# A list schedule's assumed durations are replaced, and the order that follows from them

## The chip, the core and the metric

The kernel runs on one core of a Trainium2 chip. The metric is the device time of one execution in microseconds. The core has five engines that each work through their own instruction queue in program order: TensorE (PE; its weight loads are shown as PEld), VectorE (DVE), ScalarE (ACT), GpSimd (POOL) and SyncE (SP), which issues the transfers. Nothing is reordered at run time, so the order in which the program is written down decides who waits for whom.

## What is computed

Four images of 12,480 tokens and 128 channels go through attention by way of 32 inducing rows, and each token's result goes through a two-layer ELU network with 2,048 hidden features.

```python
def mab(q, kv):                       # scale = 1/sqrt(C)
    s = scale * (q @ kv.transpose(0, 2, 1))
    a = np.exp(s - s.max(-1, keepdims=True))
    a /= a.sum(-1, keepdims=True) + 1e-09
    return a @ kv
h = mab(I, x)                         # 32 rows per image
x = mab(x, h)                         # every token again
h = x @ w_in
g = np.where(h > 0.0, h, np.exp(np.minimum(h, 0.0)) - 1.0)
out = g @ w_out
```

## The kernel before

Each of the four images is cut into 25 blocks of 512 or 480 tokens, in seven groups of two to four blocks. The network dominates. `unit` (lines 846 to 966) does two of a block's 16 feature chunks, so a block has 8 units and the run has 800, numbered through as unit 0 to 799. A unit is this chain:

- L863 on PE: two matmuls into a pair of PSUM banks, `ph`. There are three such pairs.
- L873 on ACT: `e = exp(ph - 1)`.
- L877 on DVE: the ELU's middle, written to `e` (kinds P and N) or back to `ph` (kind D).
- L887 on ACT (P and D): the rounded high part, `gh`.
- For kind P, L903 on POOL shifts `e` by one, and L907 on POOL makes the low part `gl = e - gh`. For kind D, L893 on DVE makes `gl`. For kind N there is only L903.
- L943 on PE: the second layer into a bank `po`. P and D have four matmuls with `gh` and two with `gl`. N has two matmuls in plain fp32.

A block's units are of the kinds P, D, P, D, P, D, P, N (`KINDS`); only the very first block is all N. After a block, L958 on DVE transposes `po` and SP writes it out. While image b goes through the network, the first attention step of image b+1 runs beside it: L536 makes scores, L595 and L600 their exponentials, and `gather` (L604 to L638) sums the tokens with 32-column matmuls at L614, in pieces of four (`HH`), into `ps_hh`. `attend` (L748 on) does the second attention step, one group ahead of its blocks, with L763 on PE, L787, L802 and L822 on POOL, and DMAs at L832 that put the result into one of six homes `stk`. The last image has no next image beside it.

Before the first unit there is a head of some 76 us: the first image is loaded, transposed (L1020, L1031) and gathered, `weight_steps` (L416 to L478) unpacks 64-bit weights on DVE, ACT and POOL, and a single first block is attended to (the `True` tiles, up to L814), while 64 matmuls called `warm` (L1042) fill PE.

Nothing of the order is written out by hand. Every step is registered with `add(engine, key, hold, ...)`, where `hold` is the duration that the planner assumes. `Program.order` (L167) then plays a list schedule: at each turn it takes the engine that can start first, and of that engine's steps that could start within `LOOK` ns of the earliest one it takes the one with the lowest key. `WAKE` is the wait that it assumes between an engine's work and another engine's start on it. The keys are tables of numbers (`KP`, `ATT`, `FH`, `KS`), one set for each kind of step. The resulting sequence is what each engine's queue holds.

```python
LOOK0 = 116.0
LOOKS = {'PE': 36.0, 'ACT': 105.0, 'DVE': 175.0, 'POOL': 0.0, 'SP': 3411.0}
WAKE = {"PE": 480.0, "ACT": 90.0, "DVE": 90.0, "POOL": 140.0, "SP": 60.0}
def pool_one(n):
    return 0.97 * n + 15, 45.0
def pe(n, passes=1):
    return passes * n / 2.4 + (18 if passes == 1 else 5), 165.0
```

## Time and profile before

| what | value |
|---|---|
| median of 3 runs | 1650.55 us (1650.27 to 1650.57) |
| the profiled execution | 1650.92 us, of which the span from the first to the last instruction is 1649.1 us |
| busy share of the span | PE 99%, POOL 94%, DVE 91%, ACT 90%, PEld 74% |
| granted TensorE clock | 1.00 in every slice |

A busy share is the time in which at least one instruction of the engine is shown as running. The ends of PE's instructions are modelled, and instructions overlap in the pipeline, so PE's pace is read from the distance between the starts of two matmuls, and a wait from a distance that is longer than usual. The same holds for POOL, whose instructions overlap by some 40 ns: the distance of starts is the price, not the shown duration.

### The profile page before, as it was taken

The numbers are of one execution on the slowest core, as the hardware profiler recorded it, in microseconds if no ns is written. First come the engines' busy times: TensorE is split into PE (matmuls) and PEld (weight loads), VectorE is DVE, ScalarE is ACT, GpSimd is POOL, SyncE is SP. The second block draws the span as 40 slices with busy tenths as digits, with TensorE's granted clock in tenths as the row PEclk, the third lists the DMA queues.
The fourth block names the chain that finished last, engine by engine and source line by source line (L and its number), as shares of the span: only waits on it lengthen the run. The fifth ranks groups of instructions, "written<-read, shape, count | busy, mean of one in ns | idle before, by whom it ended". The sixth has DMA issues, their size and how long they took to land.

```text
span 1649.1 us, 23463 instructions
## 1 busy us (share of the span) xinstructions
PE 1626.5 (99%) x7766; PEld 1218.8 (74%) x7766; DVE 1497.5 (91%) x1563; ACT 1485.3 (90%) x1728; POOL 1550.4 (94%) x1051
## 2 busy tenths in 40 slices
PE   6999999999999999999999999999999999999998
PEld 4667777777777777777777777778777777777886
DVE  5899989988999999898899999989989999998986
ACT  6598999899889999989989999999989999999996
POOL 3599999999899999999899999999999999999998
PEclk9999999999999999999999999999999999999999
DMA  8263322312442232321353233221122111111101
...
DMA packets 384186, 97.40 MB, mean 59 GB/s; under 512 B 364672, under 2 KB 370592, under 8 KB 383808
## 3 DMA queue, kind: packets, MB, share of 16 engines
...
## 4 chain that ended last, share of the span: by engine, by line
PE 95%; POOL 1%; DVE 1%; issue 1%; ACT 1%; DMA 1%; SPq 0%; POOLq 0%; DVEq 0%; ACTq 0%
PE po L943 67%; PE ph L863 22%; PE ps_t_False L763 2%; PE ps_s L536 2%; PE ps_hh L614 2%; POOL gl L907 1%; PE warm L1042 1%; POOL e L903 1%; DMA xm<-in_x_dram 1%; PE ps_x L1020 0%; ACT s L595 0%; DVE xT L1031 0%; PE ps_hw L729 0%; DVE e L877 0%; DVE eT L600 0%
## 5 line engine op out<-in xcount | busy, mean ns | idle before, releaser
L907 POOL TENSOR_TENSOR gl<-e,gh 128x1024 fp32r<-128x1024 f32 (+1 forms) x396 | 928.7, 2351 | 16.2
L873 ACT ACTIVATE e<-ph 128x1024 f32<-128x1024 f32 (+1 forms) x800 | 787.4, 1008 | 98.1 <-PE ph L863 93.0
L877 DVE SCALAR_TENSOR_TENSOR e<-ph,e 128x1024 f32<-128x1024 f32 (+1 forms) x503 | 593.8, 1186 | 71.8 <-ACT e L873 67.9
L903 POOL TENSOR_SCALAR e<-e 128x1024 f32<-128x1024 f32 (+1 forms) x503 | 513.7, 1031 | 33.6 <-ACT gh L887 27.8
L943 PE MATMUL po<-gh,wo_h 128*128 128x512 f32 (+1 forms) x1386 | 543.5, 392 | 0.0
L943 PE MATMUL po<-gh,wo_l 128*128 128x512 f32 (+1 forms) x1386 | 536.9, 387 | 0.0
L863 PE MATMUL ph<-stk,hw 128*128 128x512 f32 (+1 forms) x1600 | 510.8, 410 | 2.3 <-DVE e L877 2.1
L887 ACT ACTIVATE gh<-e 128x1024 fp32r<-128x1024 f32 (+1 forms) x396 | 414.2, 1046 | 13.4 <-DVE e L877 12.1
L943 PE MATMUL po<-gl,wo_h 128*128 128x512 f32 (+1 forms) x1386 | 410.4, 394 | 0.5 <-POOL gl L907 0.4
L863 PEld LDWEIGHTS ph<-stk,hw 128*128 128x128 f32 x1600 | 296.9, 188 | 111.1 <-issue 41.6
L877 DVE SCALAR_TENSOR_TENSOR ph<-ph,e 128x1024 f32<-128x1024 f32 (+1 forms) x297 | 355.4, 1197 | 18.5 <-ACT e L873 16.2
L893 DVE SCALAR_TENSOR_TENSOR gl<-ph,gh 128x1024 fp32r<-128x1024 f32 (+1 forms) x297 | 351.5, 1184 | 22.0 <-ACT gh L887 16.5
L943 PEld LDWEIGHTS po<-gl,wo_h 128*128 128x128 f32 x1386 | 256.6, 188 | 73.3 <-issue 14.3
L943 PEld LDWEIGHTS po<-gh,wo_h 128*128 128x128 f32 x1386 | 260.0, 188 | 64.3 <-issue 6.7
L887 ACT ACTIVATE gh<-ph 128x1024 fp32r<-128x1024 f32 (+1 forms) x297 | 299.4, 1008 | 8.5 <-DVE ph L877 7.7
L943 PEld LDWEIGHTS po<-gh,wo_l 128*128 128x128 f32 x1386 | 260.2, 188 | 53.5 <-issue 3.2
L943 PE MATMUL po<-e,wo_n 128*128 128x512 f32 (+1 forms) x396 | 182.1, 582 | 0.0
L943 PEld LDWEIGHTS po<-e,wo_n 128*128 128x128 f32 x396 | 74.3, 189 | 54.5 <-issue 45.8
L958 DVE STREAM_TRANSPOSE o<-po 128x512 f32<-128x512 f32 (+1 forms) x100 | 69.4, 694 | 9.8 <-PE po L943 9.3
L502 DVE STREAM_TRANSPOSE xT<-xq 128x1024 f32<-128x1024 f32 (+2 forms) x39 | 45.1, 1159 | 0.0
L822 POOL TENSOR_TENSOR alo<-aT_False,ahi 128x512 fp32r<-128x512 f32 (+3 forms) x28 | 35.5, 1267 | 0.0
L614 PE MATMUL ps_hh<-xm,eT 128*32 128x128 f32 (+2 forms) x872 | 34.3, 277 | 1.2 <-ACT s L543 0.5
...
## 6 DMA issues: line engine op xcount, KB each, us to landing
...
out_dram<-o SPq DMA_DIRECT2D x160, 60.0 KB, 1.9
...
stk<-ahi SPq DMA_DIRECT2D x80, 60.0 KB, 2.0
...
```

What stands on the lines that cost most here:

```text
L502: add("DVE", key_x, dve(n, True)[0], lambda: nc.vector.transpose(t(), xq().rearrange("p u d -> p (u d)")), r=[(xq, dq) for dq in range(4)] ...
L614: nc.tensor.matmul(ps()[c * Q : (c + 1) * Q, :C], st["e", g]()[:np_, u * Q : (u + 1) * Q], st["xm", g, u - u % UP]()[:np_, u % UP, :], sta ...
L822: add("POOL", at(), pool_two(T)[0], lambda: nc.gpsimd.tensor_sub(alo()[:np_], aT()[:np_], ahi()[:np_].bitcast(F32)), r=[(aT, 0), (ahi, 0)] ...
L863: nc.tensor.matmul(ph()[:, j, :T], st["hw"]()[:, f * P : (f + 1) * P], homes[i][:, :T], start=True, stop=True,)
L873: add("ACT", n + K["exp"][cp], act(2 * T, True)[0], lambda: nc.scalar.activation(e(), ph()[:, :, :T], AF.Exp, bias=-1.0), r=[(ph, 0)], w=[ ...
L877: add("DVE", n + K["mid"][cp], dve(2 * T)[0], lambda: nc.vector.scalar_tensor_tensor(out=ga(), in0=ph()[:, :, :T], scalar=1.0, in1=e(), op ...
L887: add("ACT", n + K["gh"][cp], act(2 * T, how == "D")[0], lambda: nc.scalar.activation(gh(), ga(), AF.Copy, bias=-1.0), r=[(g, 0)], w=[(gh, ...
L893: add("DVE", n + K["gl"][cp], dve(2 * T)[0], lambda: nc.vector.scalar_tensor_tensor(out=gl(), in0=ga(), scalar=-1.0, in1=gh().bitcast(F32) ...
L903: add("POOL", n + K["one"][cp], pool_one(2 * T)[0], lambda: nc.gpsimd.tensor_scalar(out=e(), in0=e(), scalar1=-1.0, scalar2=sign, op0=ALU. ...
L907: add("POOL", n + K["gl"][cp], pool_two(2 * T)[0], lambda: nc.gpsimd.tensor_sub(gl(), e(), gh().bitcast(F32)), r=[(e, 0), (gh, 0)], w=[(gl ...
L943: nc.tensor.matmul(po()[:, :T], w(), g_(), start=po.count == 0, stop=po.count == po.total - 1)
L958: add("DVE", n + K["o"][0], dve(T, True)[0], lambda: nc.vector.transpose(o().rearrange("p u d -> p (u d)"), po()[:, :T]), r=po.parts, w=[( ...
```

## The change

The planner's assumed durations, its assumed waits and its look-ahead get other values, and with them come other keys for the steps of the units, of the next image's attention and of the second attention step. No instruction's work, size or engine changes, and no buffer count does. What changes is only the order in each queue.

```diff
-LOOK0 = 116.0
+LOOK0 = 71.0
...
-LOOKS = {'PE': 36.0, 'ACT': 105.0, 'DVE': 175.0, 'POOL': 0.0, 'SP': 3411.0}
+LOOKS = {'PE': 0.0, 'ACT': 0.0, 'DVE': 72.0, 'POOL': 0.0, 'SP': 4748.0}
...
-FH = {'xq': 113.90625, 'xT': 47.40625, 'ps': 24.640625, 's': -68.828125, 'pm': -3.953125, 'bias': 22.75, 'xm': 48.796875, 'exp': 30.890625, 'eT': 11.796875, 'hh': 12.125, 'h': 70.96875, 'es': 197.71875, 'r': -7.734375, 'hn': 36.515625, 'hT': -31.46875, 'hw': 26.1875}
-ROOM = -31.5625
+FH = {'xq': 94.96875, 'xT': 87.6875, 'ps': 26.15625, 's': -53.15625, 'pm': -29.875, 'bias': 18.1875, 'xm': 112.9375, 'exp': 46.71875, 'eT': -1.328125, 'hh': 5.453125, 'h': 46.1875, 'es': 257.3125, 'r': -13.125, 'hn': 52.296875, 'hT': -78.703125, 'hw': 29.171875}
+ROOM = -32.1875
...
-    WAKE = {"PE": 480.0, "ACT": 90.0, "DVE": 90.0, "POOL": 140.0, "SP": 60.0}
+    WAKE = {"PE": 300.0, "ACT": 70.0, "DVE": 70.0, "POOL": 110.0, "SP": 60.0}
...
 def pool_one(n):
-    return 0.97 * n + 15, 45.0
+    return 0.97 * n + 70, 45.0
...
 def pe(n, passes=1):
-    return passes * n / 2.4 + (18 if passes == 1 else 5), 165.0
+    return passes * n / 2.4 + (16 if passes == 1 else 5), 165.0
...
-        add("ACT", n + K["exp"][cp], act(2 * T, True)[0], lambda: nc.scalar.activation(
+        add("ACT", n + K["exp"][cp], act(2 * T, True)[0] + 12, lambda: nc.scalar.activation(
...
-        add("DVE", n + K["mid"][cp], dve(2 * T)[0], lambda: nc.vector.scalar_tensor_tensor(
+        add("DVE", n + K["mid"][cp], dve(2 * T)[0] + 10, lambda: nc.vector.scalar_tensor_tensor(
...
-                add("ACT", n + K["gh"][cp], act(2 * T, how == "D")[0], lambda: nc.scalar.activation(
+                add("ACT", n + K["gh"][cp], act(2 * T, how == "D")[0] + 20, lambda: nc.scalar.activation(
```

The tables `ATT` (for the groups after the first image's first two) and `KS` (kinds a and l) change throughout, in the same manner as `FH` above.

Three places of the order, before and now. The first is PE's queue near the end of the first image, where the next image's sixth group is gathered (`ps_hh_5`, L614; the numbers in a name count the tile, and `x8` stands for eight matmuls). Before:

```order
L863 MATMUL ph_4114<-stk_169,hw_314 128x480 x2
L614 MATMUL ps_hh_5_4120<-xm_5_0_4076,eT_5_3919 32x128 x8
L943 MATMUL po_20_3997<-gl_4107,wo_h 128x480 x2
L614 MATMUL ps_hh_5_4120<-xm_5_8_4083,eT_5_3919 32x128 x4
L863 MATMUL ph_4146<-stk_169,hw_314 128x480 x2
L614 MATMUL ps_hh_5_4120<-xm_5_8_4083,eT_5_3919 32x128 x3
```

The same gather in PE's queue now:

```order
L943 MATMUL po_19_3845<-gl_3974,wo_h 128x480 x2
L614 MATMUL ps_hh_5_3999<-xm_5_0_3952,eT_5_3817 32x128 x8
L863 MATMUL ph_4014<-stk_168,hw_341 128x480 x2
L614 MATMUL ps_hh_5_3999<-xm_5_8_3961,eT_5_3817 32x128 x7
L943 MATMUL po_19_3845<-gl_3921,wo_h 128x480 x2
L863 MATMUL ph_4035<-stk_168,hw_341 128x480 x2
```

The gather stood in three pieces between matmuls of the network, and now stands in two. Over the whole queue behind the head, the gathers of images 1 to 3 stood in 41 such pieces and now stand in 35, with the same 326 matmuls of the 32-column kind.

The second place is DVE's queue in the head, just ahead of the first unit: L814 writes the home `stk_166` that the first L863 reads, and L441 to L471 are weight steps. Before:

```order
L802 TENSOR_TENSOR s_0_0_True<-s_0_0_True,sm_0_0_True 128x512
L806 STREAM_TRANSPOSE aT_0_True<-s_0_0_True 128x512
L739 TENSOR_TENSOR hw_314<-ps_hw_820,hw_314 32x512
L455 TENSOR_SCALAR w_out_190<-w_out_190 128x512
L814 TENSOR_TENSOR stk_166<-aT_0_True,stk_166 32x512
L471 SCALAR_TENSOR_TENSOR w_out_190<-w_out_190 128x512
L451 SCALAR_TENSOR_TENSOR w_part<-w_out_182,w_part 128x512
L778 STREAM_TRANSPOSE s_0_0_False<-ps_t_0_False 96x512
```

The same stretch of DVE's queue now:

```order
L455 TENSOR_SCALAR w_out_190<-w_out_190 128x512
L451 SCALAR_TENSOR_TENSOR w_part<-w_out_182,w_part 128x512
L800 RECIPROCAL sm_0_0_True<-sm_0_0_True 128x16
L739 TENSOR_TENSOR hw_341<-ps_hw_811,hw_341 32x512
L802 TENSOR_TENSOR s_0_0_True<-s_0_0_True,sm_0_0_True 128x512
L739 TENSOR_TENSOR hw_341<-ps_hw_816,hw_341 32x512
L806 STREAM_TRANSPOSE aT_0_True<-s_0_0_True 128x512
L471 SCALAR_TENSOR_TENSOR w_out_190<-w_out_190 128x512
L455 TENSOR_SCALAR w_out_182<-w_out_182 128x512
L814 TENSOR_TENSOR stk_166<-aT_0_True,stk_166 32x512
L778 STREAM_TRANSPOSE s_0_0_False<-ps_t_0_False 96x512
```

Weight steps that stood behind L814, and one L451 that stood ahead of the first block's L778, now stand between that L778 and L814.

The third place is POOL's queue at the very end, the last units of the last block (`e` and `gl` carry the same unit where a L907 names the `e` of the L903 above it). Before:

```order
L903 TENSOR_SCALAR e_15843<-e_15843 128x960
L907 TENSOR_TENSOR gl_15882<-e_15825,gh_15853 128x960
L903 TENSOR_SCALAR e_15863<-e_15863 128x960
L907 TENSOR_TENSOR gl_15911<-e_15863,gh_15890 128x960
L903 TENSOR_SCALAR e_15884<-e_15884 128x960
L907 TENSOR_TENSOR gl_15940<-e_15884,gh_15916 128x960
L903 TENSOR_SCALAR e_15923<-e_15923 128x960
L907 TENSOR_TENSOR gl_15968<-e_15923,gh_15944 128x960
L903 TENSOR_SCALAR e_15952<-e_15952 128x960
L903 TENSOR_SCALAR e_15974<-e_15974 128x960
L907 TENSOR_TENSOR gl_16002<-e_15952,gh_15984 128x960
```

The end of POOL's queue now:

```order
L907 TENSOR_TENSOR gl_15899<-e_15820,gh_15852 128x960
L903 TENSOR_SCALAR e_15880<-e_15880 128x960
L903 TENSOR_SCALAR e_15864<-e_15864 128x960
L907 TENSOR_TENSOR gl_15940<-e_15880,gh_15910 128x960
L907 TENSOR_TENSOR gl_15958<-e_15864,gh_15889 128x960
L903 TENSOR_SCALAR e_15919<-e_15919 128x960
L903 TENSOR_SCALAR e_15952<-e_15952 128x960
L903 TENSOR_SCALAR e_15975<-e_15975 128x960
L907 TENSOR_TENSOR gl_16002<-e_15919,gh_15944 128x960
L907 TENSOR_TENSOR gl_16006<-e_15952,gh_15984 128x960
```

A L907 that came directly behind the L903 of its own `e` now has another step between them, and the last two instructions are both L907. Such direct pairs stood 194 times in POOL's queue and now stand 119 times; in the last 395 us of POOL's work 19 times, and now twice.

## Rows read from the trace of the kernel before

**Rows 1.** The page: busy time of each engine (us, share of the span, instructions), and of the costliest groups POOL's L907 and L822 (count, then busy us and mean ns of one, then the idle time of the engine just before them in us).

```profile
PE 1626.5 (99%) x7766; PEld 1218.8 (74%) x7766; DVE 1497.5 (91%) x1563; ACT 1485.3 (90%) x1728; POOL 1550.4 (94%) x1051
...
L907 POOL TENSOR_TENSOR gl<-e,gh 128x1024 fp32r<-128x1024 f32 (+1 forms) x396 | 928.7, 2351 | 16.2
...
L822 POOL TENSOR_TENSOR alo<-aT_False,ahi 128x512 fp32r<-128x512 f32 (+3 forms) x28 | 35.5, 1267 | 0.0
```

**Rows 2.** The waits of PE over the whole run: who waited for whom, us in total, times, longest us. The full list has nine rows; the six left out are 0.9 us or shorter.

```profile
PE ps_ind L990 <- DMA ind<-in_inducing_dram: 11.2, 1, 11.2
PE ph L863 <- DVE e L877: 2.1, 3, 1.2
...
PE po L943 <- POOL gl L907: 0.4, 1, 0.4
```

**Rows 3.** Busy us of each engine (and instructions) in three stretches: the head, the long middle, and the last image's network to POOL's last instruction. The last three columns are the granted clock, the DMA share and GB/s.

```profile
88.00:1577.00 1489.00, 1489.00 (x6884) 1117.80 (x6883) 1374.83 (x1387) 1372.93 (x1567) 1440.34 (x943) 1.00 0.27 55
1250.00:1643.50 393.50, 392.99 (x1658) 304.94 (x1658) 354.50 (x341) 364.56 (x406) 391.84 (x254) 1.00 0.15 30
0.00:88.00 88.00, 70.75 (x599) 47.82 (x600) 66.85 (x124) 55.27 (x98) 44.67 (x67) 1.00 0.52 158
```

**Rows 4.** PE in order of time (start us, us, line, what, count): two pairs of L863 with four plain fp32 matmuls of kind N (L943, not shown) between them, then eight starts apart with 512 columns, then eleven starts apart with 480.

```profile
84.01 1.03 PE L863 MATMUL ph<-stk,hw 128*128 128x512 f32 x2
...
86.19 1.03 PE L863 MATMUL ph<-stk,hw 128*128 128x512 f32 x2
...
97.38 0.39 PE L943 MATMUL po<-gh,wo_h 128*128 128x512 f32 x1
...
99.22 0.63 PE L863 MATMUL ph<-stk,hw 128*128 128x512 f32 x2
...
1636.87 0.38 PE L943 MATMUL po<-gh,wo_h 128*128 128x480 f32 x1
...
1639.26 0.38 PE L943 MATMUL po<-gh,wo_l 128*128 128x480 f32 x1
```

**Rows 5.** PE in order of time around gathers of 32, 16, 8 and 6 matmuls at L614.

```profile
384.88 0.38 PE L943 MATMUL po<-gh,wo_l 128*128 128x480 f32 x1
385.20 1.08 PE L614 MATMUL ps_hh<-xm,eT 96*32 96x128 f32 x32
386.21 0.70 PE L943 MATMUL po<-gl,wo_h 128*128 128x480 f32 x2
386.75 0.60 PE L863 MATMUL ph<-stk,hw 128*128 128x480 f32 x2
...
405.87 0.65 PE L614 MATMUL ps_hh<-xm,eT 128*32 128x128 f32 x16
406.45 0.70 PE L943 MATMUL po<-gl,wo_h 128*128 128x480 f32 x2
407.08 0.43 PE L614 MATMUL ps_hh<-xm,eT 128*32 128x128 f32 x8
407.44 0.70 PE L863 MATMUL ph<-stk,hw 128*128 128x480 f32 x2
408.06 0.42 PE L614 MATMUL ps_hh<-xm,eT 128*32 128x128 f32 x6
```

**Rows 6.** The end of the head in order of time: first DVE, then PE. In brackets stands the idle time before and who ended it.

```profile
56.08 0.69 DVE L451 SCALAR_TENSOR_TENSOR w_part<-w_out,w_part 128x512 uint32<-128x512 uint32 x1 [1.20 <-POOL w_part L436]
...
64.54 0.68 DVE L814 TENSOR_TENSOR stk<-aT_True,stk 32x512 fp32r<-32x512 f32 x1
65.25 0.69 DVE L471 SCALAR_TENSOR_TENSOR w_out<-w_out 128x512 f32<-128x512 uint32 x1
65.86 0.68 DVE L451 SCALAR_TENSOR_TENSOR w_part<-w_out,w_part 128x512 uint32<-128x512 uint32 x1
...
68.26 2.34 DVE L877 SCALAR_TENSOR_TENSOR e<-ph,e 128x1024 f32<-128x1024 f32 x2
...
65.37 1.17 PE L863 MATMUL ph<-stk,hw 128*128 128x512 f32 x4
...
69.53 1.87 PE L863 MATMUL ph<-stk,hw 128*128 128x512 f32 x6
...
76.52 5.42 PE L943 MATMUL po<-e,w_out 128*128 128x512 f32 x12 [0.78 <-issue]
```

**Rows 7.** POOL in order of time: a stretch with 1024 columns, then one with 960, then its last instruction.

```profile
1404.40 3.07 POOL L903 TENSOR_SCALAR e<-e 128x1024 f32<-128x1024 f32 x3
1407.45 4.76 POOL L907 TENSOR_TENSOR gl<-e,gh 128x1024 fp32r<-128x1024 f32 x2
1412.18 2.05 POOL L903 TENSOR_SCALAR e<-e 128x1024 f32<-128x1024 f32 x2
...
1625.26 1.97 POOL L903 TENSOR_SCALAR e<-e 128x960 f32<-128x960 f32 x2
1627.18 2.28 POOL L907 TENSOR_TENSOR gl<-e,gh 128x960 fp32r<-128x960 f32 x1
1629.42 1.00 POOL L903 TENSOR_SCALAR e<-e 128x960 f32<-128x960 f32 x1
1630.50 2.27 POOL L907 TENSOR_TENSOR gl<-e,gh 128x960 fp32r<-128x960 f32 x1
...
1641.29 2.23 POOL L907 TENSOR_TENSOR gl<-e,gh 128x960 fp32r<-128x960 f32 x1
```

More of the change, by code (lines that the diff above doesn't have):

```diff
@@ new lines @@
+KS = {'a': {'in': [9.28125, -16.71875, -3.75, -80.3125, -16.890625, -21.015625, -57.328125, -63.453125], 'exp': [62.671875, -38.609375, 60.4375, 2.0, 12.84375, -99.921875, -43.296875, -25.296875], 'mid': [-22.640625, 11.578125, 5.671875, -39.703125, -76.578125, -64.15625, -37.375, 13.9375], 'gh': [20.828125, -2.875, -2.828125, -29.046875, 17.59375, -43.828125, 44.359375, -0.765625], 'gl': [-71.203125, 7.65625, -43.78125, -60.4375, 4.578125, 10.015625, 20.703125, -27.171875], 'one': [12.703125, 3.3125, -18.625, -29.75, -103.65625, 15.28125, 108.296875, -20.875], 'out': [14.171875, 23.453125, -2.703125, 2.03125, 18.625, 21.65625, 12.9375, -12.3125], 'late': [2.890625, -39.28125, 29.125, 3.4375, 5.53125, -20.34375, -46.078125, 57.171875], 'o': [-17.359375]}, 'l': {'in': [-13.046875, -39.265625, 8.578125, -50.265625, 1.5, -3.015625, -35.140625, -7.78125], 'exp': [3.515625, -24.03125, 12.859375, 72.703125, -36.421875, -1.03125, 9.234375, 13.65625], 'mid': [-5.171875, -27.0, 18.0625, -21.015625, -22.96875, -20.25, 2.328125, 38.171875], 'gh': [36.828125, 18.75, 48.09375, -4.0, 7.125, -65.015625, 22.234375, 50.71875], 'gl': [-63.9375, -69.796875, 33.21875, -10.484375, 14.734375, 18.25, 22.53125, 60.796875], 'one': [50.9375, -77.375, 0.65625, 43.203125, -21.90625, -3.234375, 10.078125, -7.078125], 'out': [-41.609375, 10.859375, 28.65625, 37.15625, 8.796875, -0.5, 33.765625, 27.65625], 'late': [2.9375, 26.578125, -45.5625, -20.328125, 7.8125, 19.421875, -10.59375, -55.484375], 'o': [7.890625]}, 'z': {'in': [-49.0625, -7.25, -77.828125, -4.6875, -8.5, -2.609375, -9.390625, -35.046875], 'exp': [-82.671875, -94.625, -56.84375, -143.28125, -49.328125, -67.0625, -7.78125, -82.4375], 'mid': [79.484375, -15.296875, 22.4375, 22.28125, -33.53125, 35.0, 13.546875, 146.59375], 'gh': [1.484375, 1.484375, 1.484375, 1.484375, 1.484375, 1.484375, 1.484375, 1.484375], 'gl': [11.421875, 11.421875, 11.421875, 11.421875, 11.421875, 11.421875, 11.421875, 11.421875], 'one': [-11.515625, -78.84375, 6.140625, -48.59375, 6.6875, -39.203125, -40.515625, -11.921875], 'out': [-64.203125, -5.5625, 25.53125, 60.265625, 84.53125, 17.28125, 23.796875, -17.9375], 'late': [-10.984375, -10.984375, -10.984375, -10.984375, -10.984375, -10.984375, -10.984375, -10.984375], 'o': [24.359375]}}
```

3 lines of the change are left out of this document (1 added, 2 removed).

## Prediction, made before the changed kernel was run

> **What bounds the kernel now.** I read first the busy shares, then what PE waits for, then the stretches. PE is at 99% of the span, but POOL at 94% stands close behind [rows 1], so the first question is whether PE ever waits. The list of its waits answers: 11.2 us for the first transfer, some short ones that the chains of the head explain, and 0.4 us for POOL's `gl` at the very end [rows 2]. Between 88 and 1577 us PE is busy for the whole 1489.00 us [rows 3], at the full granted clock. A busy share could still hide a slower pace, so I take the distance of starts: eight starts with 512 columns take 99.22 − 97.38 = 1.84 us, 0.230 each; eleven with 480 columns take 1639.26 − 1636.87 = 2.39 us, 0.2173 each [rows 4]. Four fp32 matmuls of kind N cost 86.19 − 84.01 − 2 × 0.23 = 1.72 us [rows 4].
>
> So three places are left in which an order can gain or lose. The head: of its first 88.00 us PE is busy for 70.75 [rows 3], and of the 17.25 idle ones 11.2 are the first transfer, which nothing in the order moves; some 6 us can move. The middle: no wait is left to remove, only a price that depends on what follows what. The end: POOL is busy for 391.84 of the last 393.50 us [rows 3] and works up to its last L907 at 1641.29 + 2.23 = 1643.52 [rows 7], just before PE's last piece. There POOL and PE are equally late, and whichever has more work behind its last wait sets the end. A gain of several per cent has no place to come from.
>
> **Gathers (L614).** No matmul is added or removed, but a switch from the network's matmuls to 32-column ones and back costs something. From the starts: 32 of them take 386.75 − 384.88 less three network matmuls of 0.217, so 1.22 us; 16 take 407.08 − 405.87 less two, 0.78; eight take 408.06 − 407.08 less two, 0.55 [rows 5]. From eight to 32, that is (1.22 − 0.55)/24 = 0.028 us for each matmul, and 0.55 − 8 × 0.028 = 0.32 us for each piece, however long. 41 pieces become 35: 6 × 0.32 = **−1.9 us**, on PE, which waits for nothing there, so it all lies on the path. It counts at the end only if POOL follows PE forward. I take it that it does: POOL's idle time sits at L907 (16.2 us [rows 1]) and in the head and middle, where it waits for what PE feeds it. The bounds are −1.9 and 0.
>
> **POOL in the last image.** Prices from the starts: L903 1.017 us with 1024 elements (3.05/3) and 0.96 with 960 (1.92/2); L907 2.365 (4.73/2) and 2.24 [rows 7]. A L907 directly behind the L903 of its own `e` starts 1.08 instead of 0.96 us after it [rows 7], so each direct pair costs 0.12 us; over the run the 16.2 us of idle before L907 spread over 194 pairs give 0.08 [rows 1]. In the last 395 us, 19 pairs become 2: that takes 2.0 us from POOL's own work. But POOL can't begin a unit before PE has. So for each L903 along the order I set the work that POOL still has from there against the work that PE still has from the same unit's L863; the unit with the largest excess of POOL ties the end. Before, it is unit 590: POOL has 75 × 1.017 + 57 × 0.96 (L903) + 60 × 2.365 + 45 × 2.24 (L907) + some 20.5 for 19 attention steps (L787 and L802 taken like L903 of their width, L822 at 1.27 [rows 1], less with 480 columns) + 19 × 0.12 = 396.5 us. PE has 870 × 0.230 + 676 × 0.2173 + 30 kind N pairs at 1.72/2 = 0.86 and 24 at 0.86 × 480/512 = 0.81 + 5.1 for gathers and attention = 397.2. The excess is −0.7. In the new order, unit 590 has −3.6, but the tie moves to unit 647: POOL 47 × 1.017 + 50 × 0.96 + 38 × 2.365 + 40 × 2.24 + 11.9 = 287.2, PE 546 × 0.230 + 580 × 0.2173 + 20 × 0.86 + 20 × 0.81 + 2.4 = 287.3 (again with gathers and attention last), an excess of −0.1. So where the fewer direct pairs relieve POOL, the units of the last image come to it in an order that gives most of that back, and the end comes **+0.6 us** later against PE's work. The prices carry an error of about 0.5% of the work between two ties, and the two sums use the same ones: I bound this at −1.3 (the pairs' relief counts, the tie at 647 does not) and +2.
>
> **The head.** Four weight steps now stand on DVE between the first block's L778 and L814: twice L451, L471 and one more L455, at 0.61 us each from start to start (65.25 to 65.86 [rows 6]) and L455 at most as much, some 2.2 in all. One L451 and the 1.20 us that DVE waited ahead of it [rows 6] leave the place before L778, of which I credit 1.4. The first L863 comes 0.7 to 0.8 later, at about 66.1 instead of 65.37 [rows 6]; `warm` matmuls cover PE until then. But L471, L451 and L455 no longer stand between L814 and the first L877, only L778 and L784: it starts at about 67.7 instead of 68.26 [rows 6]. The next L863 wait for L877 by way of the three `ph` pairs (2.1 us of waits [rows 2]), and the first L943 at 76.52 stands behind those [rows 6]. One comes later, the other earlier: **+0.1 us**, between −0.7 (L877 decides) and +1.0 (L814 decides).
>
> **PE in the middle.** Where PE would newly wait, a unit's L863 and its first L943 would have to stand closer in PE's queue than exp, middle, high part and low part take. Counted in PE's own time, the smallest such distance to `gh` goes from 4.35 to 4.22 us, one in the last image to 3.66, and once a `ph` pair is reused 1.83 instead of 2.48 us after its last reader. The nearest row for such a wait is L863's 2.1 us in three waits [rows 2], 0.7 each; one or two would be +1. I take 0, since no such distance makes PE wait before.
>
> **Sum.** −1.9 + 0.6 + 0.1 + 0 = −1.2 us. The profiled execution took 0.37 us more than the median, so I lay the sum on the median, 1650.55: **1649.3 us**. About 0.2%, 3.3 us, is what a measurement of this kernel can tell from no change, so this counts as the same.
>
> **Rivals.** *POOL alone sets the end.* If POOL's last wait for PE lies ahead of most of the saved gathers, its own work carries their gain away: 1650.55 + 0.6 + 0.1 = 1651.2. For it: 391.84 of 393.50 busy [rows 3], and the tie at 590 comes behind most gathers of the last attention step only by some ten units. Against it: POOL idles before that.
>
> *A faster head.* The first image's first gather stands earlier in PE's queue, which frees `xm` buffers and so starts later loads and `w_out` earlier. Of the 6 us of PE's idle time in the head, half could go: 1649.3 − 3 = 1646.3. For it: the head's DMA share is 0.52, against 0.27 in the middle [rows 3], so transfers matter there. Against it: DVE's chain up to L814 is full, and transfers come in the order of SP's queue.
>
> *Slower: POOL stands at unit 647.* POOL works in order; with an excess of only −0.1 there, every microsecond by which that unit's `e` comes later than PE's pace goes one to one to the end. DVE and ACT carry the other units' steps ahead of it. It decides once the lateness is above some 4.6 us (from −1.2 to +3.3), for example four L877 steps at 1.17 us (half of 2.34 [rows 6]) ahead of its own: 1649.3 + 4.7 = 1654.0. For it: new assumed durations on ACT and POOL change just these neighbours. Against it: before, PE's only wait for POOL is 0.4 us [rows 2].
>
> *PE has hidden room.* PE's weight loads are busy for 1218.8 us, 74% [rows 1], which leaves 430 us; if a new order used a tenth of them, 43 us would go, to 1607. Against it stand starts 0.230 and 0.217 us apart without a gap [rows 4], which an order can't shorten. The Trainium skill, "Perfetto Trace Analysis", section "Identifying the Most-Contended Engine", says that matmul busy time is a poor measure of how near TensorE is to its roofline and that the weight loads' busy share is the better one; by that rule there would be headroom here, and the trace's steady pace of starts disagrees that an order could use it.
>
> **How the numbers follow.** The forecast 0.53 (its own range 1647.6 to 1651), POOL alone 0.20, the faster head 0.15, slower 0.11, hidden room 0.01. Faster by over 0.2% means under 1647.25: 0.13 of the head's case, 0.04 of the forecast's lower edge, 0.01: 0.18. Slower means over 1653.85: 0.11 and 0.01 of POOL's case with a wait in the middle: 0.12. The rest, 0.70, is within. The range reaches from the head's case, 1646.2, to 1653.0, POOL's case with its bound of +2 in place of +0.6 and a little of the waits in PE's middle.
>
> **What would show it.** Gathers: 35 pieces in PE's order of time, each 0.32 us plus 0.028 for each matmul, and again no idle time of PE from 88 to 1577. POOL: idle before L907 down to some 10 us; its last two instructions both L907, PE waiting one to two microseconds between its last two `gl` pieces. Head: first L863 at about 66.1, first L943 at 76.5 ± 0.7; at 73 the faster head is right. Wrong would be the whole sum if PE showed waits for `gh` or `ph` in the middle, or if POOL idled in the last 290 us: then it stood at a unit such as 647.

## The result, and the profile after

| what | new order | kernel before |
|---|---|---|
| median | 1660.93 us (4 runs, 1659.86 to 1662.85) | 1650.56 us (1650.27 to 1651.04) |
| ratio | 1.0064, 95% interval 1.0046 to 1.0081 | |
| the profiled execution | 1659.86 us, span 1658.1 us | 1650.92 us, span 1649.1 us |

The new order is slower, by 10.4 us in the medians and 8.94 us between the two profiled executions. The forecast was no change that can be measured, 1649.3 us, and the time lies above its range. Executions of one kernel differ by up to 3 us with the clock that TensorE is granted in the head (last section); both profiled executions have the full clock there, so the 8.94 us between them are the better measure of the change.

The page of the new kernel, busy times and costliest groups in the columns of [rows 1]:

```profile
PE 1627.4 (98%) x7766; PEld 1219.3 (74%) x7766; DVE 1496.8 (90%) x1563; ACT 1483.4 (89%) x1728; POOL 1550.3 (94%) x1051
...
L907 POOL TENSOR_TENSOR gl<-e,gh 128x1024 fp32r<-128x1024 f32 (+1 forms) x396 | 928.2, 2356 | 10.3 <-PE po L943 0.2
...
L903 POOL TENSOR_SCALAR e<-e 128x1024 f32<-128x1024 f32 (+1 forms) x503 | 515.5, 1037 | 43.6 <-ACT gh L887 33.2
```

Every engine does the same work in the same busy time as in [rows 1], to within 2 us. So the time is not in any instruction but between them. The waits of PE, columns as in [rows 2]:

```profile
PE ph L863 <- DVE e L877: 3.8, 4, 1.4
PE po L943 <- POOL gl L907: 2.5, 4, 1.5
PE ph L863 <- DVE gl L893: 2.0, 3, 1.5
```

L863's wait for `gl` (L893), which reads the pair `ph` that PE wants back, is new, the one for L877 has grown from 2.1 to 3.8 us, and the one for POOL's `gl` from 0.4 to 2.5. The stretches, columns as in [rows 3], and two short ones in the last image:

```profile
0.00:88.00 88.00, 67.91 (x591) 46.71 (x592) 65.62 (x120) 52.76 (x95) 41.81 (x64) 1.00 0.49 156
88.00:1577.00 1489.00, 1485.00 (x6858) 1113.28 (x6857) 1367.67 (x1383) 1365.13 (x1561) 1433.96 (x939) 1.00 0.27 55
1250.00:1653.00 403.00, 398.47 (x1679) 307.52 (x1677) 356.22 (x344) 366.79 (x409) 394.83 (x257) 1.00 0.15 30
1368.00:1372.00 4.00, 1.23 (x5) 0.53 (x4) 4.00 (x5) 4.00 (x6) 4.00 (x4) 1.00 0.00 0
1372.00:1376.00 4.00, 4.00 (x11) 2.91 (x11) 2.57 (x3) 0.62 (x1) 4.00 (x4) 0.57 0.39 68
```

PE is idle for 4.00 us in the middle, where it had no idle time at all [rows 3]. Most of that is one place: between 1368 and 1372 PE is busy for 1.23 us, while DVE, ACT and POOL are busy throughout. The last row shows a second price: in the next 4 us PE is busy, but at a mean granted clock of 0.57, that is for most of them at the lower of TensorE's two levels, 1.2 instead of 2.4 GHz.

To place all of the 8.9 us I took, for each two neighbouring matmuls of PE, the distance of their starts less the median distance of the same kinds of neighbours in the kernel before, and summed that over stretches of 50 us. Wherever the new kernel loses visibly more than before:

| place | before | now | difference | foretold |
|---|---|---|---|---|
| head, start of the first L943 | 76.52 us | 79.02 us | +2.5 us | +0.1 |
| gathers, pieces at 0.33 us | 41 | 35 | −2.0 | −1.9 |
| 450 to 500 and 850 to 900 us | 0.16 + 0.14 | 1.26 + 1.33 | +2.3 | 0 |
| 1350 to 1400 us | 0.03 | 4.82 | +4.8 | 0 |
| 1550 us to the end | 1.48 | 2.82 | +1.3 | +0.6 |
| sum | | | +8.9 | −1.2 |

The last digit of the sum is luck: from the starts around its two waits alone, each of the two places in the third row loses 0.9 us instead of 1.1, so the account is good to about half a microsecond.

**The largest place, around unit 654.** PE in order of time, then DVE, POOL and ACT:

```profile
1367.64 0.61 PE L943 MATMUL po<-gl,wo_h 128*128 128x512 f32 x2
1369.50 0.74 PE L863 MATMUL ph<-stk,hw 128*128 128x512 f32 x2 [1.24 <-DVE e L877]
1371.77 0.94 PE L863 MATMUL ph<-stk,hw 128*128 128x512 f32 x2 [1.52 <-DVE gl L893]
1372.50 0.74 PE L943 MATMUL po<-gh,wo_h 128*128 128x512 f32 x1
1373.04 0.63 PE L943 MATMUL po<-gh,wo_l 128*128 128x512 f32 x1
1373.47 0.63 PE L943 MATMUL po<-gh,wo_h 128*128 128x512 f32 x1
...
1375.18 0.80 PE L863 MATMUL ph<-stk,hw 128*128 128x512 f32 x2
...
1376.28 0.40 PE L943 MATMUL po<-gh,wo_h 128*128 128x512 f32 x1
...
1361.56 1.23 DVE L877 SCALAR_TENSOR_TENSOR e<-ph,e 128x1024 f32<-128x1024 f32 x1 [1.34 <-ACT e L873]
...
1367.09 1.23 DVE L877 SCALAR_TENSOR_TENSOR ph<-ph,e 128x1024 f32<-128x1024 f32 x1 [0.69 <-ACT e L873]
1368.23 1.22 DVE L877 SCALAR_TENSOR_TENSOR e<-ph,e 128x1024 f32<-128x1024 f32 x1
...
1370.50 1.21 DVE L893 SCALAR_TENSOR_TENSOR gl<-ph,gh 128x1024 fp32r<-128x1024 f32 x1
1371.63 0.70 DVE L958 STREAM_TRANSPOSE o<-po 128x512 f32<-128x512 f32 x1
...
1376.08 0.71 DVE L806 STREAM_TRANSPOSE aT_False<-s_False 96x512 f32<-96x512 f32 x1 [1.50 <-POOL alo L822]
...
1374.76 1.29 POOL L822 TENSOR_TENSOR alo<-aT_False,ahi 128x512 fp32r<-128x512 f32 x1
...
1376.08 1.94 ACT L873 ACTIVATE e<-ph 128x1024 f32<-128x1024 f32 x2 [3.45 <-POOL alo L822]
```

After its last `gl` piece at 1367.64 PE has two L863 next in its queue, of units 654 and 655, and all three `ph` pairs (units 651 to 653) are still being read. L863 of 654 starts when DVE's L877 of 652 (1368.23) has ended, L863 of 655 when DVE's L893 of 651 (1370.50) has. DVE itself came late to these: it had stood for 1.34 us before L877 of 648 and 0.69 us before L877 of 651, both for ACT's `e`. By the starts it loses 1369.50 − 1367.64 − 0.46 = 1.40 us and 1371.77 − 1369.50 − 0.46 = 1.81 us. Then ten matmuls take 1376.28 − 1372.50 = 3.78 us instead of 2.30, and the pair at 1371.77 0.73 instead of 0.46: some 1.7 us at the lower clock. Together that is the 4.8 us, to within 0.2. The 3.45 us that the profile puts down to ACT's waiting for L822 come after the stalls, and the queues show another cause: this L873 is that of unit 656, which ACT has ahead of 655, and it starts right after the L863 of 656 (1375.18 + 0.80).

Why had PE nothing else? `po` and L763's result share two PSUM banks (`rooms` in the kernel). The instructions of L763 and L778 near here, first in the new kernel (count, duration in ns as min/median/max, first and last start):

```profile
L763 PE MATMUL ps_t_False<-xT,hT x8: 566/578/590, 1362.1 to 1362.6; 128*32 128x480 f32 x8
...
L778 DVE STREAM_TRANSPOSE s_False<-ps_t_False x1: 674/674/674, 1379.4 to 1379.4; 128x480 f32<-128x480 f32 x1
```

The same in the kernel before:

```profile
L763 PE MATMUL ps_t_False<-xT,hT x8: 566/578/590, 1354.9 to 1355.3; 128*32 128x480 f32 x8
...
L778 DVE STREAM_TRANSPOSE s_False<-ps_t_False x1: 674/674/674, 1356.5 to 1356.5; 128x480 f32<-128x480 f32 x1
```

Before, the attention's result held its bank for 1.6 us. Now it holds it for 17 us, because L778 stands far back in DVE's queue, behind L806, which alone waits 1.50 us for POOL's L822, and two L877. Meanwhile the only other bank belongs to the block that is ending. So the next block's first L943 can't start before L958 empties that bank at 1371.63, and the planner has it behind both L863. The `gh` of units 648 to 650 lay ready from 1366.1 on, and PE, which works in order, stands. Whether the bank or DVE's lateness costs the time is asked below.

**The head.** DVE, POOL and PE of the new kernel in order of time, to be laid beside [rows 6]:

```profile
64.85 0.71 DVE L806 STREAM_TRANSPOSE aT_True<-s_True 128x512 f32<-128x512 f32 x1
65.48 0.65 DVE L471 SCALAR_TENSOR_TENSOR w_out<-w_out 128x512 f32<-128x512 uint32 x1
66.05 0.42 DVE L455 TENSOR_SCALAR w_out<-w_out 128x512 uint32<-128x512 uint32 x1
66.50 1.67 DVE L814 TENSOR_TENSOR stk<-aT_True,stk 32x512 fp32r<-32x512 f32 x1
...
70.06 1.22 DVE L877 SCALAR_TENSOR_TENSOR e<-ph,e 128x1024 f32<-128x1024 f32 x1 [0.42 <-ACT e L873]
...
66.22 1.41 POOL L476 TENSOR_TENSOR w_out<-w_out,w_part 128x512 f32<-128x512 f32 x1 [7.82 <-DVE w_out L471]
...
63.76 3.74 PE L1042 MATMUL warm<-ident 128*128 128x128 f32 x32
68.23 1.20 PE L863 MATMUL ph<-stk,hw 128*128 128x512 f32 x4 [0.73 <-DVE stk L814]
...
79.02 3.25 PE L943 MATMUL po<-e,w_out 128*128 128x512 f32 x7 [0.68 <-issue]
```

L814 took 0.68 us before [rows 6] and takes 1.67 here. What is new beside it is POOL's L476, which L471 releases, and L471 now stands ahead of L814. The Trainium skill, "GPSIMD Engine Reference", section "1. Specifications", says that GpSimd's interfaces to SBUF are shared with VectorE and that it contends with VectorE instructions that have two SBUF inputs. L814 has two, and the trace agrees: 0.99 us more. The planner does keep POOL off while L814 runs (its `lock`), but its plan has other times than the run.

PE has a second reason to be late. Ahead of the first L863 its queue now has `warm` matmuls up to 63.76 + 3.74 = 67.50, so L863 could not have come before 67.5 even with L814 in time; in the old order it started at 65.37 [rows 6].

**The end.** POOL's last instructions and PE's last two pieces:

```profile
1648.07 4.40 POOL L907 TENSOR_TENSOR gl<-e,gh 128x960 fp32r<-128x960 f32 x2
...
1650.35 0.70 PE L943 MATMUL po<-gl,wo_h 128*128 128x480 f32 x2 [0.30 <-POOL gl L907]
1652.52 0.70 PE L943 MATMUL po<-gl,wo_h 128*128 128x480 f32 x2 [1.47 <-POOL gl L907]
```

### The profile page after: what moved, and what is told of

Same layout as the page of the kernel before. It is cut to its first block, busy times and chain, and to the rows that moved or that the text cites. A ratio compares the mean times of both kernels' runs of the same rounds, so it can differ in the third digit from the quotient of the medians.

```text
span 1658.1 us, 23456 instructions
## 1 busy us (share of the span) xinstructions
PE 1627.4 (98%) x7766; PEld 1219.3 (74%) x7766; DVE 1496.8 (90%) x1563; ACT 1483.4 (89%) x1728; POOL 1550.3 (94%) x1051
## 4 chain that ended last, share of the span: by engine, by line
PE 92%; DVE 3%; ACT 2%; DMA 1%; issue 1%; POOL 1%; SPq 0%; POOLq 0%; DVEq 0%; ACTq 0%
PE po L943 65%; PE ph L863 22%; PE ps_s L536 1%; PE ps_hh L614 1%; PE ps_t_False L763 1%; ACT e L873 1%; DVE e L877 1%; DMA xm<-in_x_dram 0%; PE warm L1042 0%; DMA xq<-in_x_dram 0%; PE ps_x L1020 0%; DVE ph L877 0%; POOL gl L907 0%; DVE xT L502 0%; ACT gh L887 0%
## 5 line engine op out<-in xcount | busy, mean ns | idle before, releaser
L907 POOL TENSOR_TENSOR gl<-e,gh 128x1024 fp32r<-128x1024 f32 (+1 forms) x396 | 928.2, 2356 | 10.3 <-PE po L943 0.2
L873 ACT ACTIVATE e<-ph 128x1024 f32<-128x1024 f32 (+1 forms) x800 | 786.1, 1011 | 107.0 <-PE ph L863 97.4
L877 DVE SCALAR_TENSOR_TENSOR e<-ph,e 128x1024 f32<-128x1024 f32 (+1 forms) x503 | 594.6, 1186 | 76.9 <-ACT e L873 73.3
L903 POOL TENSOR_SCALAR e<-e 128x1024 f32<-128x1024 f32 (+1 forms) x503 | 515.5, 1037 | 43.6 <-ACT gh L887 33.2
L943 PE MATMUL po<-gh,wo_h 128*128 128x512 f32 (+1 forms) x1386 | 545.9, 394 | 0.0
L943 PE MATMUL po<-gh,wo_l 128*128 128x512 f32 (+1 forms) x1386 | 537.1, 388 | 0.0
L863 PE MATMUL ph<-stk,hw 128*128 128x512 f32 (+1 forms) x1600 | 509.2, 410 | 6.6 <-DVE e L877 3.8
L887 ACT ACTIVATE gh<-e 128x1024 fp32r<-128x1024 f32 (+1 forms) x396 | 414.4, 1047 | 17.8 <-DVE e L877 16.8
L943 PE MATMUL po<-gl,wo_h 128*128 128x512 f32 (+1 forms) x1386 | 407.8, 392 | 2.5 <-POOL gl L907 2.5
L863 PEld LDWEIGHTS ph<-stk,hw 128*128 128x128 f32 x1600 | 294.8, 188 | 124.8 <-issue 40.6
L877 DVE SCALAR_TENSOR_TENSOR ph<-ph,e 128x1024 f32<-128x1024 f32 (+1 forms) x297 | 355.2, 1197 | 20.8 <-ACT e L873 19.9
L893 DVE SCALAR_TENSOR_TENSOR gl<-ph,gh 128x1024 fp32r<-128x1024 f32 (+1 forms) x297 | 351.4, 1183 | 19.7 <-ACT gh L887 16.3
L943 PEld LDWEIGHTS po<-gl,wo_h 128*128 128x128 f32 x1386 | 258.5, 188 | 66.6 <-issue 8.2
L943 PEld LDWEIGHTS po<-gh,wo_h 128*128 128x128 f32 x1386 | 260.3, 188 | 61.3 <-issue 3.8
L887 ACT ACTIVATE gh<-ph 128x1024 fp32r<-128x1024 f32 (+1 forms) x297 | 300.3, 1011 | 4.0 <-DVE ph L877 3.0
L943 PEld LDWEIGHTS po<-gh,wo_l 128*128 128x128 f32 x1386 | 260.5, 188 | 54.6 <-issue 4.9
L943 PE MATMUL po<-e,wo_n 128*128 128x512 f32 (+1 forms) x396 | 182.5, 583 | 0.0
L943 PEld LDWEIGHTS po<-e,wo_n 128*128 128x128 f32 x396 | 73.9, 189 | 56.5 <-issue 46.4
L958 DVE STREAM_TRANSPOSE o<-po 128x512 f32<-128x512 f32 (+1 forms) x100 | 69.3, 693 | 7.8 <-PE po L943 7.7
L822 POOL TENSOR_TENSOR alo<-aT_False,ahi 128x512 fp32r<-128x512 f32 (+3 forms) x28 | 35.5, 1267 | 1.4 <-ACT ahi L820 1.4
L614 PE MATMUL ps_hh<-xm,eT 128*32 128x128 f32 (+2 forms) x872 | 33.6, 277 | 2.0 <-ACT s L543 0.9
```

Source lines behind the costliest of these rows:

```text
L614: nc.tensor.matmul(ps()[c * Q : (c + 1) * Q, :C], st["e", g]()[:np_, u * Q : (u + 1) * Q], st["xm", g, u - u % UP]()[:np_, u % UP, :], sta ...
L822: add("POOL", at(), pool_two(T)[0], lambda: nc.gpsimd.tensor_sub(alo()[:np_], aT()[:np_], ahi()[:np_].bitcast(F32)), r=[(aT, 0), (ahi, 0)] ...
L863: nc.tensor.matmul(ph()[:, j, :T], st["hw"]()[:, f * P : (f + 1) * P], homes[i][:, :T], start=True, stop=True,)
L873: add("ACT", n + K["exp"][cp], act(2 * T, True)[0] + 12, lambda: nc.scalar.activation(e(), ph()[:, :, :T], AF.Exp, bias=-1.0), r=[(ph, 0)] ...
L877: add("DVE", n + K["mid"][cp], dve(2 * T)[0] + 10, lambda: nc.vector.scalar_tensor_tensor(out=ga(), in0=ph()[:, :, :T], scalar=1.0, in1=e( ...
L887: add("ACT", n + K["gh"][cp], act(2 * T, how == "D")[0] + 20, lambda: nc.scalar.activation(gh(), ga(), AF.Copy, bias=-1.0), r=[(g, 0)], w= ...
```

## The experiments

All but three kernels take the order as a list of the planner's step numbers. Steps, code and buffers stay, and only the sequence is another:

```diff
-            best = None
-            for e, row in there.items():
-                if not row:
+            best, step = None, self.ops[steps_in_order()[len(done)]]
+            for e, row in ((step.eng, [step]),):
+                if step.wait:
```

"Lost" means the sum over 50 us as in the table above. Places are compared by rows, and whole times by their intervals. Each ratio is to the kernel before as it ran beside that experiment, with medians of 1652.27 to 1652.69 us, not to the 1650.56 of the first table.

### Which half of the run loses: two splices

```diff
-STEPS = the new order
+STEPS = the new order up to unit 612's first L863, then the old one     (e1)
+STEPS = the old order up to unit 612's first L863, then the new one     (e2)
```

> The new order up to unit 612's first layer (the last image's second block), from there the old order. The changed kernel loses some 2.5 to 3.5 us in the head, next to nothing net in the middle, and some 6 us in the last image. Theory P (in the last image POOL has no slack; the new order makes it wait for 6.7 us in 16 places, mostly at L903 for ACT's gh, where the old order makes it wait for nothing) and theory L (PE's own stall at 1369 to 1376 us, where it runs out of ph pairs, and the half clock behind it, are the loss) both expect some 6 us back: 1654.5, between 1653 and 1656, and POOL without waits from there on. The rival that the loss comes from the head and the middle alone and is only shifted about expects over 1659.

> The old order up to unit 612's first layer, from there the new order. Theories P and L: the last image's loss alone, 1650.6 + 6 = 1656.6, between 1655 and 1658, with PE's two stalls for ph near unit 654 again. If the loss of the last image needs the new order's head and middle (another supply of finished units at its start), then under 1653.

Measured: e1 1656.76 us, 1.0027 (1.0016 to 1.0037); e2 1657.65 us, 1.0031 (1.0018 to 1.0043). Each half carries about half of the loss. e1 lies 0.8 us above its expected range; its profiled execution has a granted clock of 0.65 and 0.50 from 76 to 84 us, which costs some 2.5 us. In e1 the stretch 1350 to 1400 loses 0.03 us and 450 to 500 loses 1.32; in e2 it is 4.85 and 0.20. PE of e2:

```profile
1366.29 0.61 PE L943 MATMUL po<-gl,wo_h 128*128 128x512 f32 x2
1368.03 0.73 PE L863 MATMUL ph<-stk,hw 128*128 128x512 f32 x2 [1.13 <-DVE e L877]
1370.30 0.74 PE L863 MATMUL ph<-stk,hw 128*128 128x512 f32 x2 [1.53 <-DVE gl L893]
```

These are the same two waits, though 1300 us in another order lie ahead. So each place makes its own loss, and neither is inherited from the head.

### Is it POOL's amount of work: L903 of kind N left out in the last image

```diff
-            add("POOL", n + K["one"][cp], pool_one(2 * T)[0], lambda: nc.gpsimd.tensor_scalar(
+            add("POOL", n + K["one"][cp], pool_one(2 * T)[0], lambda: None if b == 3 and how == "N" else nc.gpsimd.tensor_scalar(
```

> The changed kernel with the same order, but without POOL's L903 of the kind N units of the last image (25 steps, some 25 us of POOL's work; the shift by one of those units is left out). Theory P: POOL is then no bound any more, so the whole loss of the last image goes, the stall near unit 654 too: some 6 us, 1654.5. Theory L: PE's stall for ph near unit 654 has nothing to do with POOL and stays, 3.1 us and some 2 us of half clock; only the 1.8 us in which PE waits for the last two gl pieces go: some 1659.

> The kernel before with the same order, without POOL's L903 of the kind N units of the last image (25 steps; their shift by one is left out). Both theories: PE waits only 0.4 us for POOL at the end and some 0.8 us shortly before, so 1649.5, between 1649 and 1650.5. If POOL were the bound of the last image in the kernel before too, by more than the trace shows, it would be under 1648.

Measured: on the new order (e4) 1661.65 us, 1.0054 (1.0042 to 1.0067), and on the old one 1649.50, 0.9988 (0.9979 to 0.9997). PE of the new order with 25 us less work on POOL:

```profile
1372.30 0.73 PE L863 MATMUL ph<-stk,hw 128*128 128x512 f32 x2 [1.24 <-DVE e L877]
1374.56 1.08 PE L863 MATMUL ph<-stk,hw 128*128 128x512 f32 x2 [1.53 <-DVE gl L893]
```

The waits are what they were, and 1350 to 1400 loses 4.78 us. So POOL's amount of work is not the cause there, and the rival "POOL stands at unit 647" falls with it. At the very end it does count a little: PE's wait of 0.30 us is gone and the last one is 1.18 instead of 1.47. On the old order POOL did cost something: the losses from 1550 to the end, 1.48 us, go down to 0.17. There the forecast's picture of POOL and PE equally late was right.

### Is it the bank, or what feeds PE

The first kernel (f1) puts L763 of group 4 behind L863 of unit 656, and the `gh` pieces of units 648, 649 and 650 ahead of L863 of 653, 654 and 655, so that this block takes the free bank. An excerpt of PE's queue:

```diff
-L763 MATMUL ps_t_4_False<-xT_8_9832,hT_3_11945 32x480 x2
-L763 MATMUL ps_t_4_False<-xT_9_9923,hT_3_11945 32x480 x2
 L943 MATMUL po_5_13279<-e_13350,wo_n 128x512 x2
...
+L943 MATMUL po_6_13421<-gh_13396,wo_h 128x512
+L943 MATMUL po_6_13421<-gh_13396,wo_l 128x512
...
+L863 MATMUL ph_13475<-stk_170,hw_8639 128x512 x2
+L763 MATMUL ps_t_4_False<-xT_8_9832,hT_3_11945 32x480 x2
```

> The changed kernel with four steps moved on PE and nothing else: L763 of the last image's fifth group, which takes one of the two po banks 17 us before DVE's L778 empties it, comes behind the L863 of unit 656, and the gh pieces of units 648, 649 and 650 (the next block's, which need that bank) come ahead of the L863 of units 653, 654 and 655. The theory that the held bank leaves PE without second-layer work near unit 654 (bank): the 3.1 us of stalls there go by 2.5 or more, the half clock behind them goes, 1660.9 - 4.5 = 1656.4. The rival that DVE and ACT are simply behind there, because PE's order gave them no unit for 2.8 us before unit 648 (feed): the wait is only moved behind the three pieces or some units on, and at least 2 us of stalls stay; over 1659.

Measured: 1660.22 us, 1.0049 (1.0035 to 1.0063). PE of this kernel:

```profile
1371.29 0.73 PE L863 MATMUL ph<-stk,hw 128*128 128x512 f32 x2 [0.42 <-DVE e L877]
...
1373.55 0.73 PE L863 MATMUL ph<-stk,hw 128*128 128x512 f32 x2 [0.60 <-DVE gl L893]
...
1375.29 0.73 PE L863 MATMUL ph<-stk,hw 128*128 128x512 f32 x2 [0.55 <-DVE gl L893]
```

The stretch loses 2.72 instead of 4.82 us. PE's waits are shorter and have work between them, and the clock stays up: 1.00 from 1368 to 1380. The bank is thus worth some 2.1 us, most of it by way of the clock. But some 2.1 us of stalls stay and the time is over 1659, which is what the expectation gave for the rival, feed. So the bank explains the slow stretch behind the stalls, and the stalls themselves only in part.

The second kernel (f4) starts unit 648 earlier: its L863 ahead of a `gh` and a `gl` piece on PE, its L873 one place ahead on ACT, so that DVE doesn't stand for 1.34 us at 1361.56. The third kernel (f5) has both edits. PE's queue in f4:

```diff
+L863 MATMUL ph_13354<-stk_169,hw_8639 128x512 x2
 L943 MATMUL po_5_13279<-gh_13317,wo_h 128x512
...
 L943 MATMUL po_5_13279<-gl_13332,wo_h 128x512 x2
-L863 MATMUL ph_13367<-stk_169,hw_8639 128x512 x2
```

> The changed kernel with two steps moved by one place each near unit 648: its L863 on PE comes ahead of the four gh matmuls of unit 644 that stand in front of it, and its exp on ACT ahead of the gh of unit 646. Nothing else moves; the bank stays held. Theory feed (DVE stood for 1.34 us before unit 648's middle because PE and ACT brought it late, and that comes back as PE's wait for ph at units 654 and 655): DVE's 1.34 us go and PE's stalls of 3.1 us there fall to 1.8 or less. Rival bank (PE has no second-layer work it may do, whatever DVE does): 3.1 us of stalls stay. In the time at most 1.5 us, 1659.5.

> The changed kernel with the two moves of the feed experiment and the four of the bank experiment. The bank moves alone left 2.06 us of stalls near unit 654 and no half clock. If feed and bank are two separate causes, the stalls fall below 1 us and the place costs under 1 us instead of 4.9. If the place is limited by DVE and ACT as a whole (what goes at one spot comes back some units on), some 2 us stay.

Measured: f4_feed 1661.84 us, 1.0057 (1.0041 to 1.0073), and f5_both 1659.29 us, 1.0046 (1.0030 to 1.0062). In f4 the 1.34 us on DVE is gone, but four smaller waits of 0.17 to 0.68 us take its place a few units on, and the stretch still loses 4.64 us. In f5 it loses 2.70, as with the bank alone. Its profiled execution, at full clock in the head, took 1657.65 us against the new order's 1659.86, also at full clock there, so the 2.1 us are seen in the time as well. Filling one hole in the feed moves it, and what makes up the last 2.7 us is not shown.

The queues name a suspect that no run moved. In the new order ACT does `gh` of 648, 649 and 650 before L873 of 651, and DVE does L877 of 652 and 653 before L893 of 651, on which L863 of 655 waits. In the old order L873 of 651 stands ahead of `gh` of 650, and L893 of 651 ahead of L877 of 653.

### The head

```diff
-L471 SCALAR_TENSOR_TENSOR w_out_190<-w_out_190 128x512
 L455 TENSOR_SCALAR w_out_182<-w_out_182 128x512
 L814 TENSOR_TENSOR stk_166<-aT_0_True,stk_166 32x512
+L471 SCALAR_TENSOR_TENSOR w_out_190<-w_out_190 128x512
 L778 STREAM_TRANSPOSE s_0_0_False<-ps_t_0_False 96x512
```

> The changed kernel with one step moved on DVE: the weight step L471 (0.57 us from start to start) stands behind L814 instead of ahead of it. Theory port: L814 took 1.67 instead of 0.68 us because POOL's L476, which waits for L471, ran beside it; so L814 takes 0.7 again and the first L863 comes 1.5 us earlier, 66.7 instead of 68.23. The rival (queue): only L471's own place counts, 0.6 us, the first L863 at 67.6. The time follows by as much, if the chain of ph behind it doesn't take it back: 1659.4 or 1660.3, hardly told apart by the time; the trace decides.

Measured: 1661.69 us, 1.0058 (1.0044 to 1.0072). DVE of this kernel:

```profile
65.07 0.71 DVE L806 STREAM_TRANSPOSE aT_True<-s_True 128x512 f32<-128x512 f32 x1
...
66.46 0.69 DVE L814 TENSOR_TENSOR stk<-aT_True,stk 32x512 fp32r<-32x512 f32 x1 [0.37 <-ACT stk L812]
```

L814 takes 0.69 us again once L471 no longer releases L476 ahead of it, so the 0.99 us are shown; in all 14 profiles of this case it takes 1.67 us where L476 starts just ahead of it (seven) and 0.68 to 0.69 elsewhere (seven). But L863 comes only 0.73 us earlier, at 67.50 and not at the expected 66.7; that is close to the rival's 67.6, though for other reasons than L471's own place. L814 starts no earlier, since it now waits 0.37 us for ACT's L812, and from its end on PE is still busy with `warm` matmuls: L863 follows the last of them without a gap. The first L943 gains 0.49 us, at 78.53, since it now waits 0.87 us for POOL's `wo_l`. The whole time shows nothing of it: this execution (h1) had the lower clock in its head, and 1350 to 1400 lost 5.86 us.

```diff
-STEPS = the new order
+STEPS = the old order up to unit 1's first L863, then the new one
```

> The old order up to the second unit's first layer, from there the new order. If the loss of the head lies in the order up to there (weight steps ahead of L814), the first L943 comes at 76.5 as before and the time falls by 2.5 us, to 1658.4. If it lies behind it (the order of the first L877 and of the second attention step), it stays at 1660.9 and the first L943 at 78 or later.

Measured (e3): 1660.45 us, 1.0048 (1.0033 to 1.0064). The first L863 starts at 64.58, the first L943 only at 77.65, between the two expected times, with a clock of 0.50 from 76 to 80 us. This mixed order also makes PE wait 1.81 us ahead of L763 for DVE's L778, which neither whole order does. So it doesn't decide, and the head's share is read from the rows of the two profiles.

### The gathers alone

On the old order, pieces of L614 joined to the piece ahead of them (g1), and a second kernel with two joins fewer (g2). Twelve and ten joins were meant; in the traces 41 pieces become 30 and 32, so it is eleven and nine:

```diff
 L614 MATMUL ps_hh_1_2388<-xm_1_0_1901,eT_1_1865 32x128 x8
+L614 MATMUL ps_hh_1_2388<-xm_1_8_1911,eT_1_1865 32x128 x8
 L943 MATMUL po_9_2308<-gl_2376,wo_h 128x512 x2
-L614 MATMUL ps_hh_1_2388<-xm_1_8_1911,eT_1_1865 32x128 x8
```

> The kernel before with 20 of the L614 steps moved on PE, each to directly behind the piece of the same gather ahead of it, so that 41 pieces become 29 and nothing else moves. By the prediction's price of 0.32 us for a piece PE saves 12 x 0.32 = 3.8 us where it never waits: 1650.6 - 3.8 = 1646.8, between 1646 and 1648. If POOL or DVE carry the gain away (POOL alone sets the end), no change, 1650.

> The kernel before with the gather pieces joined as in the first such run, but not in the second group of images 2 and 3, where joining had made PE wait 0.8 us each for POOL's e. 10 joins instead of 12: 10 x 0.33 = 3.3 us saved, some 0.7 us of small new waits in the other groups: 1650.6 - 2.6 = 1648.0, against -1.3 for all twelve. If joining anywhere makes PE wait for POOL just as much elsewhere, it stays at -1.3 or less.

Measured: g1 1650.89 us, 0.9990 (0.9982 to 0.9999), and g2 1651.13, 0.9992 (0.9983 to 1.0001). PE of g1:

```profile
404.99 0.86 PE L614 MATMUL ps_hh<-xm,eT 128*32 128x128 f32 x24
405.78 0.71 PE L943 MATMUL po<-gl,wo_h 128*128 128x480 f32 x2
406.42 0.42 PE L614 MATMUL ps_hh<-xm,eT 128*32 128x128 f32 x6
```

24 matmuls in one piece take 406.42 − 404.99 − 2 × 0.217 = 1.00 us. In the kernel before the same 24 were 16 and 8, at 0.78 + 0.55 = 1.33 [rows 5]. A join saves 0.33 us, as foretold. The Trainium skill, "TensorEngine Tiling (Array Packing)", section "Key Properties", says that a change of the tiling mode drains TensorE; the trace agrees that a switch costs, and has the price. But eleven joins should have given 3.6 us and gave 1.4: the stretch 600 to 650 lost 0.84 instead of 0.02 us, and 1000 to 1050 lost 0.80 instead of 0.05, as the steps that were moved behind the longer piece made new waits. g2 gave 1.6 where 2.6 were expected. Neither kernel is a clear gain.

### Keys without the durations

The new tables and look-ahead, but the old `WAKE`, `pool_one`, `pe` and the old holds of L873, L877 and L887:

```diff
-    WAKE = {"PE": 300.0, "ACT": 70.0, "DVE": 70.0, "POOL": 110.0, "SP": 60.0}
+    WAKE = {"PE": 480.0, "ACT": 90.0, "DVE": 90.0, "POOL": 140.0, "SP": 60.0}
...
-    return 0.97 * n + 70, 45.0
+    return 0.97 * n + 15, 45.0
...
-    return passes * n / 2.4 + (16 if passes == 1 else 5), 165.0
+    return passes * n / 2.4 + (18 if passes == 1 else 5), 165.0
```

> The new keys and look-ahead (LOOK0, LOOKS, FH, ROOM, ATT, KS) with the old assumed durations and waits. If the loss came from the keys alone, the time is that of the changed kernel, 1661; if from the durations alone, that of the kernel before, 1651. If keys and durations only fit each other as a set, it is slower than both, by 5 us or more.

Measured (f2): 1680.07 us, 1.0169 (1.0150 to 1.0189). The stretches 450 to 500 and 850 to 900 alone lose 8.21 and 7.33 us, part of it at a granted clock of 0.50 (472 to 476 and 880 to 884 us). The new keys do not fit the old durations; the old keys with the new durations were not run. So neither half of the change can be priced by itself.

## Why the prediction was wrong

**The step that failed is "PE in the middle", taken at 0 with a bound of +1.** It cost 4.8 us at unit 654 and 2.3 at the two smaller places. The part itself named the signs, a distance to `gh` of 3.66 us and a `ph` pair reused after 1.83, and then set them aside because no such distance had made PE wait before. Two things were missing. The distance in PE's own time says how long a chain may take, but the chain runs through DVE and ACT, and there its steps were queued behind others: L893 of unit 651 behind L877 of 652 and 653, and these behind an idle DVE that waited for ACT's `e` (1.34 and 0.69 us). And the banks of `po` were never looked at, though L763 in the new order keeps one for 17 us. The bound of +1 came from waits of 0.7 us each at full clock [rows 2]; the waits here were 1.4 and 1.8 us, and the lower clock behind them added 1.7 us that no row of before could show. f1 and f5 show that the bank, mostly by way of the clock, makes up 2.1 us of the 4.8. The remaining 2.7 are shown to come neither from POOL's amount of work (e4) nor from one hole in the feed (f4); which step of DVE's and ACT's order would have to move stays open. For the places near 478 and 877 us only that they come with the new order is shown, by e1 and e2. PE waits there for POOL's `gl` (0.35 and 0.38 us) and for DVE's `gl` (0.27 and 0.24). The attention's result holds a bank there too, but for 24 us instead of 20, and no run tried that.

**The head** was mis-sized, +0.1 against +2.5 us. L863 was expected at 66.1 and came at 68.23. "`warm` matmuls cover PE until then" left out that PE's own queue now has them ahead of L863 until 67.50. On DVE, the 1.4 us credited ahead of the first block's L778 did not arrive: it starts at 56.83 us instead of 56.69, since it then waits 0.76 us for PE's L763. And L814 was priced alone, while the steps moved ahead of it release POOL's L476, which runs beside it for 0.99 us more. The relief behind L814 was right in kind, but L877 then waited 0.42 us for ACT's `e`, which waits for the late L863. How the 2.5 us divide between these is not shown. With the first L943 at 79.02 the faster head is out.

**The gathers** were right in count and price: 35 pieces, 0.33 us each, −2.0. But the gain of joining was counted as if nothing else moved; g1 shows that more than half of it can go back into new waits.

**POOL's end** came as described, with two L907 last and PE waiting 1.47 us between the last pieces; the size was +1.3 instead of +0.6, inside the bound of +2. POOL's idle time ahead of L907 fell to 10.3 us, also as foretold, but it came back ahead of L903, 43.6 us where the page of the kernel before has 33.6:

```profile
L903 POOL TENSOR_SCALAR e<-e 128x1024 f32<-128x1024 f32 (+1 forms) x503 | 513.7, 1031 | 33.6 <-ACT gh L887 27.8
```

**The slower rival** had the right sign by the wrong mechanism. Its sign did appear, POOL idling late: from 1250 us to its last instruction (1652.47) it is idle for some 7.6 us, against 1.66 of 393.50 [rows 3]. But 6.4 of these are waits for ACT's `gh`, and e4 shows that less work on POOL gives nothing back near unit 654. **Hidden room** did not show: the loads' busy time hardly changed (1218.8 and 1219.3 us) while the kernel became slower.

**The assumed durations** came only in part closer to the measured ones: the new matmul of 512/2.4 + 16 = 229 ns is as near to the 230 of [rows 4] as the old 231, and the new L903 of 1063 ns is farther from the 1017 of [rows 7] than the old 1008. No run shows which of them made the order slower.
